# Retention in chunks of 64 tokens on 64x64 quarters of the array, in a kernel that fuses retention with a gated dense layer

## The chip, the cores and the metric

The kernel runs on one core of one Trainium2 chip. The metric is the device time of one execution in microseconds (us); lower is better. "The profiled span" is the length of one execution in the hardware profile; it is about 1 to 2 us shorter than the time of the same run. "The granted clock" is the share of its full clock that TensorE was allowed to use.

## The reference

Eight sequences of 576 tokens, eight heads of 64 dimensions. Each head computes causal attention without softmax, weighted by a decay, and a dense layer of 512 to 2048 to 512 with the gate h·cos(h) follows:

```python
gamma = 1.0 - 2.0 ** (-5.0 - np.arange(H))
rel   = pos[:, None] - pos[None, :]
Dmat  = np.where(rel >= 0, gamma[:, None, None] ** rel[None], 0.0)
x     = ((q @ k.T) / sqrt(64) * Dmat) @ v        # per head; x is (4608, 512)
h     = x @ w_in                                 # 512 -> 2048
out   = (h * np.cos(h)) @ w_out                  # 2048 -> 512
```

The decay factors into a power for the query and one for the key. So a block of tokens needs only its own masked scores, and one 64x64 *state* per head (the sum of k·v over all earlier tokens of the sequence) for everything before it.

## The kernel before

The 4608 tokens are taken in 36 groups of 128. One group's retention consists of *scores* (k·q), a mask on VectorE, the *own* products (v times masked scores), the *carried* products (state times q), and *states* (k·v, for the next group). A sequence has 576 = 4.5 x 128 tokens, so every ninth group holds the end of one sequence and the start of another; it needs a "mixed" mask (`tri_mix`) and a copy of v with half the rows cleared (`v_odd`).

The groups are packed into stages n0 to n9 of 512 (n1, n2: 256) tokens of the dense layer. In n3 to n9 the second dense product is Strassen's: seven products of quarter size, numbered 1 to 7, on sums of gate blocks ("gate sums", mostly on GpSimd) and of weight blocks. The work of two groups is slipped between two of these products, twice per stage. I call such a piece of work a *unit*.

```python
def scores(g, bank, ...):                  # shortened
    for hg in range(HG):
        for he in range(2):                # 64 rows x 128 keys, or 64x64 (parts=2), 128 columns
            nc.tensor.matmul(ps[i0:i1, he, hg, :], lhsT=qkT[d0:d0+D, HG+hg, i0:i1],
                             rhs=qT[d0:d0+D, hg, :], start=True, stop=True)
    mask = tri_mix if g % PER == MIX else tri
    # VectorE: ret = ps * mask

def unit7(g, bank, ...):                   # two groups between two dense products
    copy = states([g + 1, g + 2], bank)()  # 128x64 products, state adds on VectorE
    then()
    attn_out([g, g + 1], "m", nc.scalar.copy)      # own (128x64), then carried (64x64)
    if more: scores2(g + 2, put_off)
    copy(nc.scalar.copy)

# ... start-up, groups 0 to 3, before the first dense product
scores(0, "a", idle=2)
for g in range(4):
    ...
    if g + 1 < 4:
        state(g)
        transposes(g + 1, ...)             # TensorE, copied by ScalarE
        scores(g + 1, "ab"[(g + 1) % 2], idle=3)   # next scores, in another bank ...
        attn_out([g], "m", evac=nc.scalar.copy)    # ... ahead of this group's outputs
```

From group 6 on, q and k are transposed by DMA (`qkT<-qks`).

Of the kernel before, what the change touches and what calls it, by code (L numbers as in the profile page):

```python
# [17 lines left out]
def kernel(  # L18
# [28 lines left out]
    HP = P // 2  # L47
    gammas = [1.0 - 2.0 ** (-5.0 - h) for h in range(H)]
# [8 lines left out]
    S7 = 3  # L57
# [7 lines left out]
    retp = ctx.enter_context(tc.tile_pool(name="retp", bufs=4))  # L65
# [22 lines left out]
    tri = consts.tile([P, P], F32)  # L88
    tri_mix = consts.tile([P, P], F32)
    diag2 = consts.tile([P, P], F32)  # L90
# [5 lines left out]
    v_odd = consts.tile([P, 2, H, D], BF16)  # L96

    blocks4 = [consts.tile([P, HG, D], BF16, tag=f"sb{x}", name=f"sb{x}") for x in range(4)]

    tiles = {}  # L100

    def head(he, hg):
        return he * HG + hg

    def load(g, names="qkv", gate=None):

        t0 = g * P
        if g % PER == MIX:
            parts = [(0, HP, t0), (HP, P, t0 + HP)]
        else:  # L110
            parts = [(0, P, t0)]
        for name in names:
            src = {"q": q, "k": k, "v": v}[name]
            f = ld.tile([P, H, D], F32, tag="f" + name, name=f"f{name}")
            for p0, p1, t in parts:
                b, s0 = divmod(t, S)
                i = nc.sync.dma_start(
                    f[p0:p1], src[b, :, s0 : s0 + p1 - p0, :].rearrange("h s d -> s h d")
                )
                if gate is not None:  # L120
                    tc.add_manual_dep(
                        i.ins, gate.ins.name,
                        mybir.DependencyInfo(
                            mybir.DependencyClass.Sync, mybir.DependencyReason.DATA
                        ),
                        reason="weights first",
                    )
                    gate = None
            tiles["f" + name, g] = f

    def prep(g, early=False, kv_first=False):
# [22 lines left out]
        else:  # L154
            copy_v = nc.scalar.copy if g > starts[S7] // P + 17 else nc.gpsimd.tensor_copy
            copy_v(vb, fv)  # L156
            if c == MIX and g > PER:
                copy_v(v_odd[HP:, g // PER % 2], fv[HP:])
# [28 lines left out]
    def scores(g, bank, idle=0, parts=1, put_off=None):  # L187
        qks, vb, qkT, qT = tiles["a", g]
        ps = psum.tile([P, 2, HG, P], F32, tag=bank, name="sc")
        warm(ps[:, 0].rearrange("p b i -> p (b i)"), idle)  # L190
        for hg in range(HG):
            for i0 in range(0, P, P // parts):
                for he in range(2):
                    d0, i1 = he * D, i0 + P // parts
                    nc.tensor.matmul(  # L195
                        ps[i0:i1, he, hg, :],
                        lhsT=qkT[d0 : d0 + D, HG + hg, i0:i1],
                        rhs=qT[d0 : d0 + D, hg, :],
                        start=True,
                        stop=True,  # L200
                    )
        ret = retp.tile([P, 2, HG, P], BF16, tag="ret", name="ret")
        mask = tri_mix if g % PER == MIX else tri
        tiles["ret", g] = ret

        def masked():
            nc.vector.tensor_tensor(  # L207
                out=ret.rearrange("p a b i -> p (a b) i"),
                in0=ps.rearrange("p a b i -> p (a b) i"),
                in1=mask.unsqueeze(1).to_broadcast([P, H, P]),  # L210
# [3 lines left out]
        if put_off is None:  # L214
            masked()
        else:
            put_off.append(masked)

    def state(g):
        c = g % PER  # L220
        if c == PER - 1:
            return
        qks, vb, qkT, qT = tiles["a", g]
        fresh = c in (0, MIX)
        if fresh:
            tiles["stps"] = psum.tile([P, HG, P], F32, tag="st", name="st")
        ps = tiles["stps"]
        p0 = HP if c == g == MIX else 0
        vs = v_odd[:, g // PER % 2] if c == MIX and g > PER else vb
        for hg in range(HG):  # L230
            nc.tensor.matmul(
                ps[:, hg, :],
                lhsT=qks[p0:, 1, 2 * hg : 2 * hg + 2, :].rearrange("s h d -> s (h d)"),
                rhs=vs[p0:].rearrange("s (a b) d -> s b a d", a=2)[:, hg],
                start=(fresh and hg == 0),
                stop=(c in (MIX - 1, PER - 2) and hg == HG - 1),
                skip_group_check=True,
            )
        sb = stp.tile([P, HG, P], BF16, tag="sb", name="sb")
        nc.vector.tensor_tensor(  # L240
            out=sb,
            in0=ps,
            in1=diag2.unsqueeze(1).to_broadcast([P, HG, P]),
            op=ALU.mult,
        )
        tiles["sb", g + 1] = sb

    def states(gs, bank="st"):



        gs = [g for g in gs if g < NG and g % PER != PER - 1]
        if not gs:
            return lambda: (lambda *_: None)
        apart = bank == "b"
        if apart:
            two = psum.tile([P, 2, 2, HG, D], F32, tag=bank, name="st")
            ps = two[:, :, 0]
        else:
            ps = psum.tile([P, len(gs), HG, D], F32, tag=bank, name="st")  # L260
        for x, g in enumerate(gs):
            qks, vb, qkT, qT = tiles["a", g]
            vs = v_odd[:, g // PER % 2] if g % PER == MIX else vb
            for hg in range(HG):
                for he in range(2):
                    nc.tensor.matmul(
                        ps[he * D : he * D + D, x, hg, :],
                        lhsT=qks[:, 1, 2 * hg + he, :],
                        rhs=vs[:, head(he, hg), :],
                        start=((apart or x == 0) and hg == 0),  # L270
                        stop=((apart or x + 1 == len(gs)) and hg == HG - 1),
                        skip_group_check=True,
                    )

        def copy(run=nc.vector.tensor_copy):
            for g in gs:
                s, sb = tiles.pop(("s32", g)), blocks4[g % 4]
                run(sb, s)
                tiles["sb", g + 1] = sb

        def add():
            for x, g in enumerate(gs):
                s = stp.tile([P, HG, D], F32, tag="s32", name="s32")
                if g % PER in (0, MIX):
                    nc.vector.tensor_copy(s, ps[:, x])
                else:
                    nc.vector.tensor_tensor(out=s, in0=ps[:, x], in1=tiles["s32"], op=ALU.add)
                tiles["s32"] = tiles["s32", g] = s
            return copy

        return add

    def attn_out(gs, bank, evac=nc.vector.tensor_copy):


        two = len(gs) == 2
        ps = psum.tile([P, DG, len(gs), P], F32, tag=bank, name="ov")

        def out_of(h, x, n=P):
            return ps[h % 2 * D : h % 2 * D + D, h // 2, x, :n]  # L300

        def carried():
            for h0 in (0, 2) if two else (0,):
                for x, g in enumerate(gs):
                    c = g % PER
                    if c == 0:
                        continue
                    qT = tiles["a", g][3]
                    sb = tiles["sb", g]
                    n = HP if c == MIX else P  # L310
                    heads = [(he, h0 + j) for j in range(2) for he in range(2)]
                    if not two:
                        heads = [(he, hg) for hg in range(HG) for he in range(2)]
                        heads.sort(key=lambda u: head(*u))
                    for he, hg in heads:
                        h = head(he, hg)
                        r = slice(he * D, he * D + D)
                        k = r if two else slice(0, P)
                        nc.tensor.matmul(  # L319
                            out_of(h, x, n),  # L320
                            lhsT=sb[k, hg, r] if sb.shape[2] == P else sb[k, hg, :],
                            rhs=qT[k, hg, :n],
                            start=(not two and h < 2),
                            stop=(two and h % HG >= 2),
                            skip_group_check=True,
                        )

        def own():
            for x, g in enumerate(gs):
                vb = tiles["a", g][1]  # L330
                ret = tiles.pop(("ret", g))
                for h in range(H):
                    nc.tensor.matmul(  # L333
                        out_of(h, x),
# [547 lines left out]
```

## Time and profile before

| | before |
|---|---|
| time, median of the first 3 runs | 299.27 us (298.97 to 299.58) |
| profiled span | 296.6 us |
| TensorE matmul busy | 285.2 us, 96% |
| VectorE, GpSimd, ScalarE busy | 70%, 67%, 46% |
| granted clock | 1.00 |

Of the waits of TensorE before, two lines (engine and tile waiting, what it waited for, us in total, times, longest):

```profile
PE sc L195 <- DMA qkT<-qks: 1.2, 1, 1.2
PE o L515 <- DVE ot L557: 1.0, 4, 0.4
```

The start-up before, from the timeline of TensorE (start, busy us, line, operation, operands, count, and in brackets the idle time before with what ended it); the lines between are left out. Scores of groups 0 to 3 begin at 9.77, 12.12, 14.52, 16.72, and the first dense product, `h`, at 17.61:

```profile
9.77 0.45 PE L195 MATMUL sc<-qT,qkT 64*128 64x128 bf16 x8 [0.25 <-ACT qkT L177]
12.12 0.40 PE L195 MATMUL sc<-qT,qkT 64*128 64x128 bf16 x8
...
17.61 1.05 PE L365 MATMUL h<-xT,w_in_sb 128*128 128x256 bf16 x8
...
19.49 0.71 PE L365 MATMUL h<-xT,w_in_sb 128*128 128x256 bf16 x5
```

One unit before, in stage n6, from the same view. It runs from 193.79 to 195.28:

```profile
193.79 0.32 PE L266 MATMUL st<-vb,qks 128*64 128x64 bf16 x8
193.94 0.62 PE L333 MATMUL ov<-ret,vb 128*64 128x128 bf16 x16
194.49 0.42 PE L319 MATMUL ov<-qkT,sb 64*64 64x128 bf16 x16
194.73 0.62 PE L195 MATMUL sc<-qkT 64*64 64x128 bf16 x32
195.28 1.92 PE L515 MATMUL o<-w_out_sb,gT 128*128 128x256 bf16 x16
```

The last transposing DMA that n5 needs was issued at 160.91, and the unit whose scores need it began at 163.55. The lead was 2.6 us. The scores of the unit's second group, which need this DMA, began at 164.94, and the DMA had landed at 164.90. The issue and the scores, from the timelines of the DMA queue (SPq) and of TensorE (the second group is the second half of the scores' line):

```profile
160.91 1.29 SPq L167 DMA_TRANSPOSE qkT<-qks  x1
164.62 0.74 PE L195 MATMUL sc<-qkT 64*64 64x128 bf16 x32
```

### The profile page before, as it was taken

Reading aid. Unit: us, or ns where it says so; the run is one execution under the profiler, and the core shown is the slowest. Engines: PE = TensorE matmul, PEld = TensorE weight load, DVE = VectorE, ACT = ScalarE, POOL = GpSimd, SP = SyncE. Lnnn points to the kernel's source line nnn. Section 1 sums busy time; section 2 is a strip of 40 time slices with the busy share of each in tenths; the row PEclk is TensorE's granted clock in tenths of the full one; section 3 lists DMA queues with packets and bytes.
Section 4 is the critical chain, followed back from the end, with each engine's and each line's share of the span. In section 5 each row is a group of like instructions: output and inputs, shape, how many; then the busy total and the mean of one; then the engine's idle time right before and its main releaser. Section 6 shows DMA issues by size and latency. Waiting matters only on the chain. (4 is left out here: it accounts for less than half of the span.)

```text
span 296.6 us, 7311 instructions
## 1 busy us (share of the span) xinstructions
PE 285.2 (96%) x3091; PEld 195.6 (66%) x3113; DVE 208.9 (70%) x245; ACT 135.9 (46%) x167; POOL 199.7 (67%) x163
## 2 busy tenths in 40 slices
PE   7899999999989999999999999999999999999995
PEld 3478646848568887468745784488448844884594
DVE  6677647564669995688758975897589758935873
ACT  3656432605236532663256355636464446425620
POOL 2750056544445789999999998599859935970583
PEclk9999999999999999999999999999999999999999
DMA  8999999999999999999999999997850260021013
GB/s 208 213 210 207 210 197 201 210 210 232 201 160 232 199 243 231 216 283 160 198 217 254 212 213 221 200 223 194 180 140 2 73 144 0 2 81 62 0 38 106
DMA packets 154304, 50.28 MB, mean 170 GB/s; under 512 B 140832, under 2 KB 153248, under 8 KB 154272
## 3 DMA queue, kind: packets, MB, share of 16 engines
q1 hardware_dynamic: 149504, 45.10, 77.9%
q0 software_dynamic: 4224, 4.19, 8.5%
q8 instruction: 24, 0.39, 0.5%
q10 hardware_dynamic: 544, 0.52, 0.5%
q14 instruction: 8, 0.07, 0.1%
HBM read 36.70 MB, written 9.44 MB: 156 GB/s over the span
## 5 line engine op out<-in xcount | busy, mean ns | idle before, releaser
L443 POOL TENSOR_TENSOR gs<-gT 128x1024 bf16<-128x1024 bf16 x51 | 107.1, 2131 | 36.1 <-DVE gs L443 35.5
L365 PE MATMUL h<-xT,w_in_sb 128*128 128x512 bf16 (+2 forms) x820 | 126.8, 313 | 1.3 <-DVE xT L350 0.7
L374 DVE TENSOR_TENSOR gT<-h,cosh 128x1024 bf16<-128x1024 f32 x72 | 87.9, 1223 | 45.5 <-ACT cosh L373 43.0
L373 ACT ACTIVATE cosh<-h,half_pi 128x1024 f32<-128x1024 f32 x72 | 80.2, 1114 | 66.9 <-PE h L365 66.9
L365 PEld LDWEIGHTS <-w_in_sb 128*128 128x128 bf16 x832 | 75.9, 98 | 49.5 <-issue 1.0
L140 POOL TENSOR_TENSOR qks<-fq,gq 128x512 bf16<-128x512 f32 x32 | 34.2, 1068 | 40.0 <-DMA fq<-in_q_dram 33.7
L515 PEld LDWEIGHTS <-gs 128*128 128x128 bf16 x576 | 53.9, 98 | 9.5 <-issue 1.7
L140 POOL TENSOR_TENSOR qks<-fk,gk 128x512 bf16<-128x512 f32 x35 | 37.7, 1076 | 9.4 <-DMA fk<-in_k_dram 8.8
L207 DVE TENSOR_TENSOR ret<-sc,tri 128x1024 bf16<-128x1024 f32 x32 | 38.1, 1215 | 2.7 <-PE sc L195 2.7
L515 PE MATMUL o<-ws,gs 128*128 128x256 bf16 (+1 forms) x352 | 38.8, 268 | 0.1
L382 PE MATMUL o<-w_out_sb,gT 128*128 128x512 bf16 x120 | 28.9, 380 | 0.5 <-issue 0.2
L515 PE MATMUL o<-w_out_sb,gs 128*128 128x256 bf16 x224 | 26.3, 272 | 1.0 <-DVE ot L557 1.0
L515 PE MATMUL o<-w_out_sb,gT 128*128 128x256 bf16 x224 | 26.3, 273 | 0.0
L535 DVE TENSOR_TENSOR ot<-o,ot 128x512 f32<-128x512 f32 (+2 forms) x25 | 14.9, 603 | 13.9 <-PE o L515 13.8
L515 PEld LDWEIGHTS <-gT 128*128 128x128 bf16 x224 | 21.5, 98 | 4.2
L350 ACT CAST xT<-ov 128x1024 bf16<-128x1024 f32 (+1 forms) x18 | 16.5, 917 | 16.0 <-PE ov L319 13.9
L443 DVE TENSOR_TENSOR gs<-gT 128x1024 bf16<-128x1024 bf16 (+1 forms) x18 | 21.1, 1187 | 0.3
L382 PEld LDWEIGHTS <-gT 128*128 128x128 bf16 x128 | 11.8, 98 | 12.5
L156 POOL CAST vb<-fv 128x512 bf16<-128x512 f32 x22 | 13.8, 628 | 5.1 <-DMA fv<-in_v_dram 3.3
L562 ACT COPY ot<-o 128x512 f32<-128x512 f32 x7 | 4.1, 586 | 20.2 <-PE o L515 20.2
L392 ACT COPY ot<-o 128x512 f32<-128x512 f32 x8 | 4.7, 588 | 18.5 <-PE o L382 18.4
L195 PEld LDWEIGHTS <-qkT 64*64 64x64 bf16 (+1 forms) x512 | 9.0, 105 | 6.1 <-ACT qkT L177 2.3
(70 smaller groups left out, 176.1 us busy)
## 6 DMA issues: line engine op xcount, KB each, us to landing
out_dram<-ot SPq DMA_DIRECT2D x35, 256.0 KB, 4.0
fk<-in_k_dram SPq DMA_DIRECT2D x32, 256.0 KB, 5.1
fv<-in_v_dram SPq DMA_DIRECT2D x32, 256.0 KB, 5.1
fq<-in_q_dram SPq DMA_DIRECT2D x30, 256.0 KB, 4.5
w_in_sb<-in_moe_w_in_dram POOLq DMA_DIRECT2D x4, 512.0 KB, 8.9
w_out_sb<-in_moe_w_out_dram POOLq DMA_DIRECT2D x4, 512.0 KB, 16.3
fq<-in_q_dram SPq DMA_DIRECT2D x8, 128.0 KB, 4.0
fk<-in_k_dram SPq DMA_DIRECT2D x8, 128.0 KB, 4.1
```

The lines of the kernel that those rows point to most:

```text
L140: eng.tensor_tensor(out=qks[:, m].rearrange("p (b a) d -> p a b d", a=2), in0=f.rearrange("p (a b) d -> p a b d", a=2), in1=by[:, c, :].re ...
L156: copy_v(vb, fv)
L195: nc.tensor.matmul(ps[i0:i1, he, hg, :], lhsT=qkT[d0 : d0 + D, HG + hg, i0:i1], rhs=qT[d0 : d0 + D, hg, :], start=True, stop=True,)
L207: nc.vector.tensor_tensor(out=ret.rearrange("p a b i -> p (a b) i"), in0=ps.rearrange("p a b i -> p (a b) i"), in1=mask.unsqueeze(1).to_br ...
L350: evac(tiles["x", n][:, :, t0 : t0 + len(gs) * P], ps.rearrange("p c x i -> p c (x i)"))
L365: nc.tensor.matmul(ps[:, j, :], lhsT=w_in_sb[:, dg, (et + j) * P : (et + j + 1) * P], rhs=xT[:, dg, c0 : c0 + w], start=(dg == 0), stop=(d ...
L373: nc.scalar.activation(cosh, ps, ACTF.Sin, bias=half_pi, scale=1.0)
L374: nc.vector.tensor_mul(gT[:, et : et + m, c0 : c0 + w], ps, cosh)
L382: nc.tensor.matmul(ps, lhsT=gT[:, et, tsi * P : (tsi + 1) * P], rhs=w_out_sb[:, et, :], start=(et == 0), stop=(et == ET - 1),)
L443: i = (nc.vector if on_dve else nc.gpsimd).tensor_tensor(out=tiles["gs", n, x][:, e0:e1], in0=i0, in1=i1, op=op_)
L515: nc.tensor.matmul(dst[i], lhsT=lhs[:, e, j * P : (j + 1) * P], rhs=rhs[:, e, c0:c1], start=(x in (3, 4, 1, 7) and e == 0 and (i == 0 or l ...
L535: pend.append(lambda: nc.vector.tensor_tensor(out=out_, in0=in0, in1=in1, op=op_))
```

## The change

Intent: 576 is nine times 64. In chunks of 64 tokens no chunk straddles two sequences, so the mixed masks go. A mask covers 64 by 64, so VectorE masks half as many elements. And every product is 64x64 with 64 columns: four of them run in the four quarters of the array, and the tile shape no longer changes within a unit. Between products that use different rows for the same output an order must be kept; this is done with an empty instruction (nop) on ScalarE. The diff, cut to its core:

```diff
-    def scores(g, bank, idle=0, parts=1, put_off=None):
+    def scores(gs, bank="a", idle=0):
+        for y, g in enumerate(gs):
+            for hg in range(HG):
+                for x in range(2):
+                    for he in range(2):
+                        nc.tensor.matmul(ps[half(x), he, y, hg, :],
+                            lhsT=qkT[half(he), HG + hg, half(x)],
+                            rhs=qT[half(he), hg, half(x)], start=True, stop=True)
...
+    def retention(gs, bank="m", evac=nc.scalar.copy, between=lambda: None):
...  (cut: the products are sorted into three parts: carried, own, carried of the other row half)
+        for p, part in enumerate(parts):
+            for h, x, y, lhsT, rhs in part:
+                i = nc.tensor.matmul(ps[half(h % 2), x, y, h // 2, :], lhsT=lhsT, rhs=rhs, ...)
+                if turn is not None:
+                    fence(i, turn, "other rows")
+                    turn = None
+            if p == 0:
+                if i is not None:
+                    turn = nc.scalar.nop()
+                    fence(turn, i, "other rows")
+                between()                  # scores and states of the next pair
...
     # start-up
-    scores(0, "a", idle=2)
     for g in range(G4):
+        masked = scores([g], idle=2)
...
+        add, copy = states([2 * g, 2 * g + 1])
+        add(0, 1)
+        copy(0, 1, nc.vector.tensor_copy)
+        masked()
+        add(1)
+        copy(1)                            # ScalarE
         if g + 1 < G4:
-            state(g)
-            transposes(g + 1, "nn", only=(1,))
-            scores(g + 1, "ab"[(g + 1) % 2], idle=3)
-            attn_out([g], "m", evac=nc.scalar.copy)
+            transposes(g + 1, (("n", "st")[g % 2],) * 2, only=(1,))
+            retention([g])
...
+    def unit(g, bank="m", more=True, then=lambda: None, finish=at_once):
+        found = []
+        more = more and g + 2 < NG
+        retention([g, g + 1], bank,
+            between=lambda: found.extend(ready([g + 2, g + 3])) if more else None)
+        then()
+        if more:
+            finish(*found)
```

So a steady unit's order changes from states, own, carried, scores to carried, scores, states, own, carried. One gate sum of the stages n5 to n8 also moves from GpSimd to VectorE.

## The prediction

> **What bounds the kernel.** The busy table gives TensorE matmul 285.2 of 296.6 us (96%); VectorE 70%, GpSimd 67%, ScalarE 46%. The waits of TensorE add up to about 6 us; the granted clock is 1.00. So after the prelude (17.6 us, latency bound) TensorE time is kernel time. The dense products (110 ns per 256 columns) are not touched.
>
> **What retention costs now.** In the timeline the work of one steady pair of 128-token groups stands at 193.79 to 195.28: states 0.15 to 0.27, own 0.55, carried 0.25, scores 0.55. It delays TensorE by about 1.58 us between the products around it; 18 pairs, some 27 us. Starts in the trace: four 64x64 matmuls of 128 columns every 56 ns; four of 64 columns (mixed groups, one sample) 28 ns; their weight loads also 28 to 31 ns. Each change of tile shape shows about 0.1 us extra, three to four per pair. The Trainium skill, "TensorEngine Tiling (Array Packing)", Key Properties, says that a mode change drains TensorE; the gaps agree.
>
> **What the change does to TensorE.** Per pair 32 scores, 32 states, 32 own, 32 carried, all 64x64 with 64 columns: 4 x 8 quads x 31 ns = 1.0 us, plus two mode changes: estimate 1.25 us against 1.58, so 0.33 saved per pair where nothing waits; at best 6 us.
>
> **What takes it back.**
> - The fence through a ScalarE nop should pass once earlier ScalarE work is dispatched (Trainium skill, "PSUM — Partial Sum Buffer", Engine vs sequencer instructions). With scores and states between (0.5 us) it is free; without, I estimate 0.33 us of stall (groups 3, 4, 5, some pairs).
> - States now take bank b directly after product 3 of a stage: they must wait for VectorE's last gate product (193.30 to 194.52). Estimate 0.3 us in each of the last four stages with retention, which eats that unit's gain.
> - In the prelude retention(g) precedes scores(g+1): 0.3 us later.
> - Pair 10/11 waits for its transposing DMA (1.16 us now); more work follows that wait: 0.25 us lost.
>
> **What else is gained.** Product 2's wait for VectorE's "ot" (0.16 to 0.38 us per stage, 1.0 in all) goes, since one mask (1.21 us) per pair leaves VectorE, against two more state adds (0.42) and a gate sum from GpSimd (2.13 there). The waits of scores for "s" (0.45) and states for "ot" (0.28) go. VectorE falls by about 10 us, GpSimd by 6 to 10; neither is critical.
>
> **Sum.** Last four stages with retention 1.7, 117 to 148 us 1.0, 85 to 117 us 1.2, before that 0, prelude -0.3: 3.5 us saved. Predicted 295.8 us (-1.2%), 8 in 10 within 293.0 to 298.4. Faster by over 2%: 0.12; within 2%: 0.85; slower by over 2%: 0.03.
>
> **What would show it.** Scores, states, own, carried: mean start pitch 7 to 8 ns per matmul, no 128x64 forms left. TensorE busy down by 4 to 6 us. Waits list: states waiting for the gate product (L374), 0.3 us each; own products waiting for ScalarE only where nothing lies between; product 2's wait for "ot" gone. First h matmul at about 18 us.
>
> **What would make it wrong.** Quads of 64 columns held by weight loads (over 40 ns a quad takes all the gain); the nop queuing behind running ScalarE work (Sin 1.11 us), up to 1 us per unit and then slower; or bank b free early, 1.2 us more gain.

## More of the kernel before

A function `feed`, called after each output store, issues on the queue of SyncE the loads of q, k, v some groups ahead, and the transposing DMAs, one behind the other. GpSimd scales q and k and casts v before that.

From the page of the kernel before: the busy table, TensorE's clock and the DMA's busy share in 40 slices of the span, and the queue that carries instructions.

```profile
span 296.6 us, 7311 instructions
PE 285.2 (96%) x3091; PEld 195.6 (66%) x3113; DVE 208.9 (70%) x245; ACT 135.9 (46%) x167; POOL 199.7 (67%) x163
PEclk9999999999999999999999999999999999999999
DMA  8999999999999999999999999997850260021013
q8 instruction: 24, 0.39, 0.5%
```

TensorE is busy nearly always, so it bounds the kernel. But look at the DMA row too: it stands at 90% or more in 26 of the first 27 slices.

The busy times by stretch, of n4 and n5 before (length, then busy us and count of TensorE, weight loads, VectorE, ScalarE, GpSimd; clock; DMA busy share; GB/s).

```profile
116.87:147.85 30.98, 30.36 (x352) 19.97 (x353) 23.39 (x25) 13.61 (x16) 30.07 (x24) 1.00 1.10 215
147.85:178.09 30.24, 29.75 (x336) 19.94 (x337) 23.16 (x24) 15.92 (x21) 28.84 (x24) 1.00 1.12 225
```

GpSimd, 67% busy over the span, is busy 30.07 of 30.98 us in n4.

## The result, and the profile after

| | before | after |
|---|---|---|
| time, median (range) of 4 runs each | 299.42 us (298.97 to 301.03) | 310.01 us (309.73 to 310.21) |
| ratio of the fast runs | | 1.0343, 95% interval 1.0303 to 1.0383 |
| profiled span | 296.6 us | 308.1 us |
| TensorE matmul busy | 285.2 us | 284.3 us |
| granted clock, mean | 1.00 | 0.971 |

All runs of this table gave correct results. Ratios here and below are the mean time of one kernel's fast runs over that of the other's in the same rounds, so they are not quite the ratio of the medians quoted. The change is 3.4% slower; 310 lies far outside the range predicted.

The same lines of the page, after (the DMA row, again full, is left out):

```profile
span 308.1 us, 9160 instructions
PE 284.3 (92%) x3982; PEld 194.6 (63%) x4006; DVE 197.2 (64%) x259; ACT 147.0 (48%) x184; POOL 190.3 (62%) x158
PEclk9857999999999999999999979999999999999999
q8 instruction: 31, 0.51, 0.8%
```

TensorE's busy time did not rise; its idle time did, by 12.4 us (23.8 against 11.4). VectorE and GpSimd have less to do, as intended. The clock row has two dips that were not there. And the instruction queue moved 31 packets instead of 24. Of the waits of TensorE after, those that bear on what follows:

```profile
PE sc L190 <- DMA qkT<-qks: 5.7, 2, 3.7
PE ov L300 <- ACTq L314: 2.4, 4, 0.8
PE o L492 <- POOL gs L422: 2.3, 4, 1.0
PE h L344 <- DVE ret L202: 1.6, 1, 1.6
PE st L234 <- DVE gT L353: 0.6, 3, 0.2
```

To place the loss I took from both traces the start of each stage, that is of its first weight load for a dense product (to within 0.1 us). "Full h" is the point from which the dense products of n0 run without a break (19.49 before). All in us of the profiled runs:

| | start to full h | n0 | n1 | n2 | n3 | n4 | n5 | n6 | n7 | n8 |
|---|---|---|---|---|---|---|---|---|---|---|
| before | 19.49 | 29.32 | 17.47 | 18.62 | 31.97 | 30.98 | 30.24 | 29.69 | 29.75 | 29.10 |
| after | 26.85 | 29.42 | 17.34 | 18.38 | 32.60 | 32.42 | 34.14 | 29.03 | 29.03 | 28.78 |
| difference | +7.36 | +0.10 | -0.13 | -0.24 | +0.63 | +1.44 | +3.90 | -0.66 | -0.72 | -0.32 |

So there are three parts: a gain of 1.70 in n6 to n8, a loss of 7.36 in the start-up, and a loss of 5.97 in n3 to n5. (n9 holds no unit and hardly moved; the columns sum to +11.4 of the 11.5 us between the spans.)

**The gain.** One unit after, n6, the counterpart of the unit shown above:

```profile
206.91 0.32 PE L300 MATMUL ov<-qkT,sb 64*64 64x64 bf16 x16
207.05 0.43 PE L190 MATMUL sc<-qkT 64*64 64x64 bf16 x32
207.69 0.37 PE L234 MATMUL st<-vb,qks 64*64 64x64 bf16 x20 [0.21 <-DVE gT L353]
...
207.95 0.43 PE L300 MATMUL ov<-ret,vb 64*64 64x64 bf16 x28
208.20 0.33 PE L300 MATMUL ov<-qkT,sb 64*64 64x64 bf16 x16
208.46 1.92 PE L492 MATMUL o<-w_out_sb,gT 128*128 128x256 bf16 x16
```

The states wait 0.21 us for the last gate product, and this unit takes 208.46 - 206.91 = 1.55 us, about what it took before. The other unit of the stage waits for nothing and takes 1.23 us, from its first product to the next dense one, where one before took some 1.5:

```profile
213.80 0.28 PE L300 MATMUL ov<-qkT,sb 64*64 64x64 bf16 x10
215.03 1.70 PE L492 MATMUL o<-ws,gs 128*128 128x256 bf16 x14
```

Product 2 no longer waits for "ot". This part works as predicted.

**The start-up.** From the same timeline, lines between left out:

```profile
10.04 0.50 PE L190 MATMUL sc<-qT,qkT 64*64 64x64 bf16 x16 [0.24 <-ACT qkT L172]
12.72 0.32 PE L300 MATMUL ov<-ret,vb 64*64 64x64 bf16 x16 [0.74 <-ACTq L314]
13.59 0.35 PE L190 MATMUL sc<-qT,qkT 64*64 64x64 bf16 x16 [0.16 <-ACT qkT L172]
16.37 0.43 PE L300 MATMUL ov<-ret,vb 64*64 64x64 bf16 x16 [0.67 <-ACTq L314]
...
21.89 0.43 PE L190 MATMUL sc<-qT,qkT 64*64 64x64 bf16 x16 [0.36 <-ACT xT L328]
24.14 1.86 PE L344 MATMUL h<-xT,w_in_sb 128*128 128x256 bf16 x8 [1.61 <-DVE ret L202]
```

Of the rounds left out, the scores begin at 17.80 and the own products at 20.45. One round from scores to scores took 2.2 to 2.4 us before; now it takes 3.6, 4.2 and 4.1. Own products wait each time for the nop ("ACTq" is ScalarE's queue). The first group of eight dense products takes 1.86 us instead of 1.05: the clock is halved. In the record of the clock it stands at 0.5 from 13.7 to 27.4 us. (The expectations of e1 and e7 below put this stretch at 6.8 to 20.5 us; that was misread.)

ScalarE at the first of these nops:

```profile
12.65 0.41 ACT L258 CAST sb<-s 128x256 bf16<-128x256 f32 x1 [2.14 <-DVE s L252]
```

The nop stands behind the cast of the second state. The cast begins at 12.65, and the own products at 12.72, while the cast still runs until 13.06. At the other two nops it is the same: the trace has the nops at 12.66, 16.31 and 20.39, and the casts' starts at 12.65, 16.30 and 20.34. So the nop passes as soon as the cast has been *dispatched*. This agrees with the Trainium skill, "PSUM — Partial Sum Buffer", Engine vs sequencer instructions, which says that the sequencer waits only for earlier instructions to be dispatched. The prediction cited that sentence and drew the wrong conclusion from it: the cast could not be dispatched before VectorE's fourth operation of the round (the add of the second state, 12.20 to 12.61) was done. A nop behind an instruction that waits for another engine waited for that engine too.

One more link stands in the last line of TensorE's timeline above. The first dense product waits 1.61 us for VectorE's mask of group 3. The code says why: all scores of the new start-up use bank "a", which the first dense product takes too; before, they alternated between "a" and "b", and no such wait is in that trace.

**The transposing DMA in n5.** TensorE after, around the longest wait (before, the scores of the counterpart began at 164.62 without a wait):

```profile
172.73 0.32 PE L300 MATMUL ov<-qkT,sb 64*64 64x64 bf16 x16
172.87 0.30 PE L190 MATMUL sc<-qkT 64*64 64x64 bf16 x16
176.91 0.32 PE L190 MATMUL sc<-qkT 64*64 64x64 bf16 x16 [3.74 <-DMA qkT<-qks]
...
178.01 3.36 PE L492 MATMUL o<-w_out_sb,gT 128*128 128x256 bf16 x16
```

The DMA that the second half of these scores needs was issued at 172.80 after (160.91 before), as the timeline of the DMA queue says:

```profile
172.80 1.38 SPq L162 DMA_TRANSPOSE qkT<-qks  x1
```

The unit began at 172.73. The lead of 2.6 us had become -0.1. The wait costs more than itself: after 3.7 us of idling the clock halves again, and the next product takes 3.36 us instead of 1.91. That queue hardly stands still: from the first transposing DMA to this one no gap is longer than 1.3 us in either kernel. The first one was issued 5.4 us later than before (55.58 against 50.17), and the stretch from there to this one was 6.5 us longer (117.2 against 110.7), as much as its loads of q, k and v held the queue longer (65.8 against 59.3 us). So the issue was late in part because the start was, in part because the loads were slower.

And the new units need the DMA sooner. In the old order the second group's scores began 1.39 us after the unit (164.94 against 163.55). In the new order they would have begun after 0.44 us (176.91 less the wait of 3.74 is 173.17, against 172.73). So of the wait of 3.74 us, 0.95 comes from the new order within the unit and 2.7 from the lost lead.

**Gate sums.** The same stretches as shown before, after (n4 and n5):

```profile
124.59:157.01 32.42, 30.04 (x481) 19.71 (x481) 24.64 (x30) 15.53 (x18) 29.72 (x24) 1.00 1.09 200
157.01:191.15 34.14, 30.30 (x417) 20.29 (x417) 20.80 (x26) 16.66 (x21) 31.84 (x27) 0.95 1.16 216
```

GpSimd works 29.7 us in n4, as before, but with its inputs later: in this stretch it waits 2.0 us for loads of q and v (0.3 us before). A GpSimd without slack then hands its gate sums over late, and the last products of n3 and n4 wait 0.2 to 1.0 us each, four times, 2.3 in all.

### The profile page after: what moved, and what is told of

It is laid out like the page before. It is cut to its first block, busy times and chain, and to the rows that moved or that the text cites. A ratio compares the mean times of both kernels' runs of the same rounds, so it can differ in the third digit from the quotient of the medians.

```text
span 308.1 us, 9160 instructions
## 1 busy us (share of the span) xinstructions
PE 284.3 (92%) x3982; PEld 194.6 (63%) x4006; DVE 197.2 (64%) x259; ACT 147.0 (48%) x184; POOL 190.3 (62%) x158
## 4 chain that ended last, share of the span: by engine, by line
PE 66%; POOL 9%; DMA 8%; DVE 5%; issue 4%; ACT 4%; SPq 2%; DVEq 0%; ACTq 0%; POOLq 0%
PE h L344 34%; PE o L492 18%; PE o L361 7%; POOL gs L422 7%; DMA fq<-in_q_dram 5%; DMA qkT<-qks 3%; PE ov L300 3%; ACT cosh L352 2%; PE idle L180 2%; POOL qks L137 2%; DVE gT L353 2%; PE st L234 1%; SPq L120 1%; PE sc L190 1%; DVE s L252 1%
## 5 line engine op out<-in xcount | busy, mean ns | idle before, releaser
L422 POOL TENSOR_TENSOR gs<-gT 128x1024 bf16<-128x1024 bf16 x47 | 98.6, 2128 | 48.5 <-DVE gs L422 48.5
L258 ACT CAST sb<-s 128x1024 bf16<-128x1024 f32 (+3 forms) x20 | 16.6, 832 | 39.3 <-DVE s L252 34.3
L252 DVE TENSOR_TENSOR s<-st,s 128x256 f32<-128x256 f32 x56 | 23.6, 422 | 14.6 <-PE st L234 13.5
L512 DVE TENSOR_TENSOR ot<-o,ot 128x512 f32<-128x512 f32 (+2 forms) x32 | 19.7, 622 | 18.8 <-PE o L492 15.4
L492 PE MATMUL o<-w_out_sb,gT 128*128 128x256 bf16 x224 | 28.1, 282 | 0.7 <-DVE gT L353 0.7
L331 ACT CAST xT<-ov 128x512 bf16<-128x512 f32 x30 | 16.1, 589 | 21.4 <-PE ov L300 21.0
L202 DVE TENSOR_TENSOR ret<-sc,tri 128x1024 bf16<-128x1024 f32 (+1 forms) x21 | 22.3, 1064 | 5.1 <-PE sc L190 5.1
L422 DVE TENSOR_TENSOR gs<-gT 128x1024 bf16<-128x1024 bf16 (+1 forms) x22 | 18.8, 879 | 0.4
L512 DVE TENSOR_TENSOR ot<-ot,o 128x512 f32<-128x512 f32 x14 | 9.6, 687 | 7.4 <-ACT ot L542 4.5
```

The source lines that it names most:

```text
L202: nc.vector.tensor_tensor(out=ret[:, :, : len(gs)].rearrange("p a g b i -> p a (g b) i"), in0=ps[:, :, : len(gs)].rearrange("p a g b i -> ...
L252: nc.vector.tensor_tensor(out=s32[:, y], in0=kv[c], in1=tiles["s32"], op=ALU.add)
L258: run(sb[:, y0:y1], s32[:, y0:y1])
L331: evac(xT[:, x], ps[:, x])
L422: i = (nc.vector if on_dve else nc.gpsimd).tensor_tensor(out=tiles["gs", n, x][:, e0:e1], in0=i0, in1=i1, op=op_)
L492: nc.tensor.matmul(dst[i], lhsT=lhs[:, e, j * P : (j + 1) * P], rhs=rhs[:, e, c0:c1], start=(x in (3, 4, 1, 7) and e == 0 and (i == 0 or l ...
```

## The experiments

Theory 1: the start-up's loss is a serial chain, TensorE states, VectorE add, ScalarE cast, nop, own products, and the next scores behind all that. Rival 1: the halved clock makes it long. Theory 2: the losses in n3 to n5 (n2 to n5 where the start-up is the old one) come from the loads. The change has about 1800 more TensorE instructions, these are fetched by DMA in packets, and the packets hold up a load stream that has no slack. Rival 2: these losses come from the late start alone, or from the new units themselves (their order, as just seen, does take a part).

All twelve kernels gave correct results. The kernel before, run beside them, had medians of 299.25 to 299.61 us (one of its runs, beside e4, e7 and e12, was slow and is left out of the ratios).

### e1: the second cast on VectorE; e2: scores ahead; e3: both

e1 takes the cast away from ScalarE, e2 puts the scores of the next group ahead of the retention of this one as the kernel before had it (with it the scores alternate between two banks again, behind three idle products instead of two), e3 does both.

```diff
 e1, e3:
-        copy(1)
+        copy(1, run=nc.vector.tensor_copy)
 e2, e3:
+    nxt = scores([0], idle=2)
     for g in range(G4):
-        masked = scores([g], idle=2)
+        masked = nxt
...
-        add, copy = states([2 * g, 2 * g + 1])
+        add, copy = states([2 * g, 2 * g + 1], ("n", "st"))
...
-            transposes(g + 1, (("n", "st")[g % 2],) * 2, only=(1,))
+            to = "ba"[g % 2]
+            transposes(g + 1, to + to, only=(1,))
+            warm(psum.tile([P, 512], F32, tag="m", name="idle"), 3)
+            nxt = scores([g + 1], to)
             retention([g])
```

> The changed kernel with one line altered: in the prelude the bf16 cast of the second state runs on VectorE instead of ScalarE. Theory A (the nop and the next qkT copy queue on ScalarE behind that cast, which waits for the fourth VectorE op): the wait of own products for the nop falls from 0.7 us per group to under 0.2, scores(3) start at about 19.5 instead of 21.9 us, first full h at about 24.3 instead of 26.85, total 307.0 to 307.8 (changed: 310.0). Rival B (it is the order, retention(g) ahead of scores(g+1)): under 0.7 us gained, 309.4 or more. Rival C (the halved clock from 6.8 to 20.5 us is the cause): unchanged, 310.

> The changed kernel with the kernel before's order in the prelude: transposes and scores of the next group ahead of retention of this one; the ScalarE cast stays. Theory A: the next qkT copy still queues behind the cast on ScalarE, so scores(g+1) gain little by the order: 1 to 2 us gained, 308 to 309. Rival B (order alone): most of the 7.4 us of the prelude comes back, 302.5 to 304.

> Both edits. Both theories: the prelude is as short as before's within 1.5 us, full h stream from 20 to 21 us instead of 26.85. If the later losses (stages at 92 to 191 us: +0.6, +1.4, +3.9 us) are only a result of lateness of the prelude, they go too and the total is 293 to 297, faster than before (299.4). If they come from the changed steady part itself, the total is 302 to 304.

| | time, us | ratio to before | full h at | end of n0 at |
|---|---|---|---|---|
| after | 310.01 | 1.0343 (1.0303 to 1.0383) | 26.85 | 56.27 |
| e1 | 309.75 | 1.0357 (1.0300 to 1.0414) | 25.58 | 56.32 |
| e2 | 309.43 | 1.0346 (1.0303 to 1.0389) | 25.56 | 55.89 |
| e3 | 307.35 | 1.0278 (1.0246 to 1.0310) | 22.52 | 52.58 |

The expectations missed in size. Full h was to come at 24.3 us in e1 and at 20 to 21 in e3. No total lies in a range given for theory A (theory 1 here), e3's lies outside both of its ranges, and e1's, taken alone, would fit rival B. (e1 and e2 have two runs each.) So the chain is read from the traces, not from the totals. Each edit alone moves full h by 1.3 us, and in the total neither shows. Together they move it by 4.3 us. That is what two links of one serial chain do: take one away and the other stands in its place. In e1 the own products wait for VectorE's mask instead (0.9 us, three times), in e2 the scores wait for ScalarE's copy of the keys (3.1 us, four times). The first dense product's wait for the mask is still there in e1 (1.6 us) and gone in e2 and e3, which alternate the banks. e1's own gain is then lost in n0 (30.74 us against 29.42): the half-clock stretch lasted 17.1 us there and reached into the dense products. e3's profile (of the fastest of its six runs, 304.36 us) has nearly the same losses in n3 to n5, 5.1 us, with 4.2 us of waits for transposing DMAs and 2.2 us for gate sums, though full h comes 4.3 us earlier. So most of them do not come from the start-up's length; e6 tests this better.

### e4: the nop on VectorE

```diff
-            retention([g])
+            retention([g], by=nc.vector)      # turn = by.nop() in place of nc.scalar.nop()
```

> The kernel after, with one difference: in the start-up alone, the empty instruction that separates the carried products from the own products stands on VectorE instead of ScalarE. Theory (the empty instruction waits its turn behind ScalarE's cast of the second state, 0.74, 0.67 and 0.77 us of TensorE wait): those three waits fall to 0.1 to 0.4 us, but the copy of the next transposed keys on ScalarE still stands behind the same cast, so the first full dense product moves only 0.5 to 1.3 us earlier than 26.85. Rival (the fence itself, wherever it stands, drains TensorE): waits and start-up unchanged. In either case the time stays above 308.

308.13 us, 1.0285 (1.0249 to 1.0321). The three waits fell to 0.35, 0.27 and 0.28 us and are now put down to VectorE's mask. So the nop's place cost the wait, not the fence as such. But full h came at 26.53, only 0.3 us earlier, less than the theory's 0.5 to 1.3: the time went into the next link. I expected the direction and over-estimated the size.

### e7: idle products against the halved clock

```diff
-            retention([g])
+            retention([g], between=lambda: warm(
+                psum.tile([P, 512], F32, tag=("st", "n")[g % 2], name="idle"), 4))
```

> The kernel after, with four idle 128x512 products put into the gap between carried and own products of each of the three start-up retentions (0.86 us of TensorE work at full clock). It asks what the granted clock of 0.5 between 6.8 and 20.5 us costs. If the clock is what makes the start-up long, the half-clock period vanishes or shrinks and the first full dense product comes 1.5 us or more earlier than 26.85. If the chain through ScalarE and VectorE is what makes it long, the clock rises but the start-up stays within 0.7 us of 26.85, or gets longer by what the idle products overshoot the gap.

The clock stays at 1.0 through the whole start-up; the page's clock row, which can be held against that of the kernel after:

```profile
PEclk9997999999999999999999779999999999999999
```

The first dense product comes at 23.71 instead of 24.14, 0.4 us earlier, and full h 1.3 us earlier, because those eight products now take 1.03 us. This fits neither of my bounds. But at the end of n0 only 0.3 us is left of it (56.00 against 56.27): a half-clock stretch of 3.4 us came all the same, now in the first dense products, where 12 ran at 0.21 us apiece instead of 0.11. So rival 1 falls as the main cause. The clock costs something, but with a full clock the start-up is still over 6 us longer than before.

The kernel as a whole was 305.11 us, 1.0200 (1.0160 to 1.0240), nearly 5 us faster than the change, though the start-up cannot account for that. (The profiled run is the slowest of the four, 306.94 us.) I come back to that below.

### e6: the old start-up with the new rest

The start-up of before, up to group 3, with its own scores, states and outputs; everything after it as in the kernel after (some 80 lines of the old kernel put back, with its 128x128 mask and `diag2`).

> The changed kernel with the first four groups done as in the kernel before (128-token chunks, masks and state bank as there), all later groups in 64-token chunks. Full h stream at 19.4 to 19.8 us as before. Theory L (the later losses are only lateness of the prelude): stages at or below before's, total 293 to 296. Theory I (TensorE's 1500 extra instructions are fetched by DMA in 16 KB packets, 30 instead of 24, and each stalls the saturated load stream by 1.3 us): the stage after the fifth (30.24 us in before, 34.1 in changed) still loses 2 to 4 us on the transposing DMA, total 297 to 300.

Two of the four runs were slow (307.68 and 305.99); the fast ones are 303.71 and 301.41, ratio 1.0114 (1.0046 to 1.0183). Both are slower than the 297 to 300 that I expected with theory I (theory 2 here), and the four runs lie far apart. Full h came at 19.44, as before. So the whole 7.4 us belong to the new start-up. The later losses stay, and the waits of its TensorE show them undiluted:

```profile
PE sc L192 <- DMA qkT<-qks: 7.9, 3, 4.0
PE o L560 <- POOL gs L490: 3.0, 4, 1.0
```

The two long waits for transposing DMAs stand in n2 (3.96 us) and n5 (3.47 us). Against before, n2, n4 and n5 lose 3.2, 1.4 and 2.9 us. Stages n6 to n8 are as in the kernel after (29.03, 29.03, 28.78). So the middle stages lose with the old start-up too.

### e5: the old kernel, started late

The first half of rival 2. The kernel before, with 30 idle products (6.45 us) before the dense part:

```diff
+    warm(psum.tile([P, 512], F32, tag="n", name="idle"), 30)
     for g in (4, 5):
         prep(g)
```

> The kernel before with 30 idle matmuls of 512 columns (6.5 us) put ahead of its first h matmul, nothing else. If lateness by itself upsets the later stages (loads held back, then late), the total rises by clearly more than 6.5 us: 308 to 311, and the trace shows new waits for transposing DMAs or gate sums between 90 and 190 us. If lateness alone is harmless, 305.5 to 306.3 and the later stages keep their lengths (31.9, 31.0, 30.2 us).

306.85 us, 1.0260 (1.0209 to 1.0311), between my two ranges. The profiled span grew by 7.7 us, of which 6.45 is the delay. Beyond it, n3 and n4 took 2.8 us more (33.57 and 32.17 us against 31.97 and 30.98, with 2.3 us of waits for VectorE's gate product), and n2 took 1.35 us less, as its wait for a DMA vanished. But n5 took 30.08 us, and no wait for a late transposing DMA appeared there: the unit began 7.9 us later than before (171.44), the DMA was issued 4.8 us later (165.75), so the lead grew. A late start alone does not make n5's wait.

### e8: the old kernel with more TensorE instructions

The test of theory 2 itself: the kernel before, its dense products of 256 and 512 columns cut into two halves. The same arithmetic, the same loads, the same retention.

```diff
+            k = 2 if w > P else 1
             for dg in range(DG):
-                nc.tensor.matmul(ps[:, j, :], lhsT=..., rhs=xT[:, dg, c0 : c0 + w], ...)
+                for z in range(k):
+                    nc.tensor.matmul(ps[:, j, z * w // k : (z + 1) * w // k], lhsT=..., 
+                        rhs=xT[:, dg, c0 + z * w // k : c0 + (z + 1) * w // k], ...)
...                                            # and likewise in mm2
```

> The kernel before with most dense products cut into two half-width matmuls: 1664 more TensorE instructions, the same arithmetic, no other change. By the pitches in the trace (216, 109, 56 ns for 512, 256, 128 columns) this costs TensorE 2.3 us. Theory I: 30 or 31 instruction packets instead of 24, load issues take 4 to 6 us longer between the first and the 18th transposing DMA, and a new wait for that DMA shows near 165 us: total 303 to 306. Rival (instruction count is harmless): total 301 to 302.3, no such wait.

304.08 us, 1.0167 (1.0126 to 1.0208), profiled span 303.1. From its page and its waits:

```profile
PE 291.4 (96%) x3945; PEld 251.4 (83%) x3945; DVE 211.4 (70%) x245; ACT 136.0 (45%) x167; POOL 199.0 (66%) x163
q8 instruction: 30, 0.49, 0.7%
...
PE sc L195 <- DMA qkT<-qks: 2.4, 2, 1.7
PE o L520 <- POOL gs L448: 1.0, 2, 0.7
```

The old kernel, without any change of its retention, gets the symptoms of the new one: 30 packets, a wait of 1.71 us for a transposing DMA in n5 (33.17 us long instead of 30.24), gate sums that come late in n4. The cut products cost something on TensorE too: in the stages without such waits (n0, n1, n6 to n8) the kernel lost 0.9 us in all. In n2 to n5 it lost 5.5 us (18.39, 33.00, 32.78, 33.17). There TensorE's idle time rose by some 2.2 us and its busy time by 3.4, of which about 1.7 can be the clock, which stands at 0.5 for 3.4 us from 171.0 us on, just behind the wait in n5. So I estimate that about 3.9 of the 5.5 us are waiting and what it brings, and 1.6 the cut products' own cost. The profiled run is the slowest of four; two others had a granted clock of 0.999 and 1.000 and still took 303.74 and 303.32 us, so the slowdown of 4 us does not hang on the halved clock.

What the packets do can be counted in the traces. Between the first and the 18th transposing DMA of a kernel stand the loads of q, k and v that decide when those DMAs are issued. I took how long the queue was held by each load (half of them between 0.6 and 1.1 us), how many packets of instructions started in between, and how long the stretch lasted:

| | matmuls and weight loads, page | packets in all | packets in the stretch | loads held over 1.9 us | all loads, us | stretch, us |
|---|---|---|---|---|---|---|
| before | 6204 | 24 | 10 | 2 | 59.3 | 110.7 |
| e5 | - | 24 | 10 | 3 | 60.8 | 113.5 |
| after | 7988 | 31 | 14 | 7 | 65.8 | 117.2 |
| e6 | - | 30 | 13 | 5 | 63.6 | 116.7 |
| e8 | 7890 | 30 | 14 | 5 | 63.2 | 116.7 |
| e7 | - | 31 | 14 | 2 | 62.6 | 115.3 |

A packet is 16 KB (0.39 MB / 24). The Trainium skill, "Runtime: NRT & Kernel Launch", Instruction fetch mechanics, says that instructions are refilled in blocks of 16 KiB, 256 instructions each, through DMA. The traces agree: 6204 / 256 = 24.2 and 7988 / 256 = 31.2, against 24 and 31 packets. The same section calls the cost of a block mostly hidden. For the loads that share the DMA engines it is not: over all fourteen kernels, of 245 loads with a packet started between 1.0 us before and 1.5 us after their own start, 59 were held over 1.9 us. Of 655 without one, 1 was. With the packets' times shifted by 3 us either way, the same count gives 4 of 290 and 2 of 292. The mean load took 1.26 us near a packet and 0.84 elsewhere. I estimate from each kernel's own means that the loads near packets held the queue for 9.8 us more than they would have elsewhere in the kernel after, for 4.8 before, but for only 6.8 in e8. Over all kernels that is 0.4 to 0.8 us a packet, not the 1.3 that I expected in e6. So packets can explain most of the longer stretch of the kernel after (6.5 us) and about half of what e8's loads took longer (3.9 us).

e7 shows how much hangs on where the packets fall. It has as many of them as the change, but a few dozen more instructions in its start-up (9208 in all against 9160) shift all later packets against the stream. One load in the queue of the kernel after, and the same one in e7 (another, at 48.90 after, went from 2.30 to 0.85 us):

```profile
58.98 2.67 SPq L120 DMA_DIRECT2D fv<-in_v_dram  x1
```

```profile
57.07 0.92 SPq L120 DMA_DIRECT2D fv<-in_v_dram  x1
```

Its wait in n2 is gone (16.27 us against 18.38), that in n5 is 2.8 us. That these hits were missed *because* the packets shifted is the reading that I find likely. No run moves the packets and nothing else, so this much is argued, not shown. And it does not reach n5: with two loads held instead of seven, n5 still took 34.28 us, no less than the 34.14 of the kernel after, as a half-clock stretch of 6.8 us came with the wait. So held loads alone do not make n5's loss.

### e9 to e12: can the saturated stream be relieved?

If transposing DMAs stand behind loads that are not needed yet, those loads can be issued later. e9 is e6 with loads kept three groups ahead instead of five at four places:

```diff
+            if (n, r) in ((0, 3), (1, 0), (1, 1), (1, 2)):
+                ahead = prepared + 3
             while loaded < min(NG, prepared + LD, ahead):
```

> As e6_old_prelude, and around the fourth and fifth stage the loads are issued three groups ahead instead of five, so that the two transposing DMAs that the fifth stage waits for stand earlier in their queue. If theory I and the queue order hold, the wait of 3 to 4 us is gone and the total is 2 to 4 us below e6_old_prelude, 293 to 296, faster than before; if the wait has another cause, it is within 1 us of e6_old_prelude.

300.69 us, 1.0028 (0.9968 to 1.0089): the best version of the new retention, and level with before; the 293 to 296 that I expected were missed. n5 fell from 33.17 to 29.08 us; its wait is gone, with the number of instructions unchanged. Its DMA was issued at 159.62, 8.7 us before the unit began. This shows that with an early issue n5 loses nothing; it is 1.2 us shorter than before. But n6 rose by 1.6 us (three short waits) and n4 to 33.25, where the products wait 3.0 us for gate sums.

e10 adds two more reliefs to e9: the preparation of pair 10/11 at the end of n2, where its DMA has landed, and one gate sum of n4 on VectorE. It holds loads back at three places only.

```diff
-            if (n, r) in ((0, 3), (1, 0), (1, 1), (1, 2)):
+            if (n, r) in ((0, 3), (1, 0), (1, 1)):
...
-            (S7, 1, 4), (last, 1, 0), (last, 2, 4)
+            (S7, 1, 4), (S7 + 1, 2, 4), (last, 1, 0), (last, 2, 4)
...
-            todo = [..., (25, lambda: unit(8))]
+            todo = [..., (25, lambda: unit(8, more=False)), (31, lambda: first(*ready([10, 11])))]
```

> e9_old_prelude_loads_later with three reliefs: loads held back only up to the fifth transposing DMA of that stretch; scores and states of groups 10 and 11 issued at the end of the third stage instead of inside the unit of groups 8 and 9 (their transposing DMA was waited for 3.6 us there); one gate sum of the fifth stage on VectorE instead of GpSimd (GpSimd sums were waited for 3.0 us there). If those three waits are the rest of the loss and the 64-token units keep their gain: 294.5 to 297, faster than before by 0.8 to 1.6%. If the saturated DMA stream only moves the waits elsewhere: 298.5 to 301.

A miss: 302.79 us, 1.0119 (1.0088 to 1.0149). n2's wait fell (3.6 to 1.4 us) and n4 came down to 30.71. But VectorE got the mask and four state adds just before the first gate products of n3, and n3 rose to 35.14. The traces show the chain of the start-up again: VectorE was done with the adds at 87.26, ScalarE's cast of the states waited for them until 87.29, the cosine of n3's first products stood behind the cast (88.72), the gate product behind the cosine (89.87), and the dense products of 91.15 waited 1.74 us for the gate product, and a half-clock stretch of 3.4 us came with it.

And with the fourth place not held back, n5's wait returned (2.7 us in two waits, n5 33.47).

e11 is the control: the kernel before with the same three places held back.

> The kernel before with only the later loads of e10. It waits for no transposing DMA of that stretch, so the relief alone should buy nothing: within 1 us of before (299.3). If it is faster by 1.5 us or more, part of e10's gain is not the chunks' doing.

299.39 us, 1.0001 (0.9976 to 1.0026). Later loads alone buy nothing where nothing is late.

e12 is e9 with the one gate sum of n4 on VectorE.

> The kernel e9 (start-up of before, rest of after, four load batches later) with one GpSimd gate sum of stage n4 (product 2, second half) put on VectorE, which in e10 took n4 from 33.25 to 30.71. Prediction: n4 30.5 to 31.5, the other stages as in e9 (n5 29.1, n2 21.4); in all 297.5 to 299.5, that is 0.0 to 0.6 per cent below before. If saturated engines only pass the wait on, n4 gains and n5 or n6 lose as much, and the time stays at 300 to 301.

A miss again: 300.71 us, 1.0048 (1.0012 to 1.0084). n4 came to 31.87, n5 stayed at 29.18, and n6 stood at 30.94. No version of the new retention that I tried beats the kernel before.

## Why the prediction was wrong, point by point

- *"After the prelude TensorE time is kernel time"* failed, and it is the step on which the rest stood. TensorE's busy time was to fall by 4 to 6 us. It fell by 0.9, because it rose by 2.7 in the start-up, much of which ran at half clock, and the kernel became 10.6 us slower. There was a second limit just below the first: a load stream almost without gaps from 50 to 170 us, whose lead of 2.6 us in n5 was all used, and GpSimd at 97% in n4 (30.07 of 30.98 us). I read the shares over the whole span (GpSimd 67%) and wrote "neither is critical". Stage by stage it is.
- *The term "prelude -0.3"*, a loss of 0.3 us, measured 7.4. The term counted one reordering. It left out that own products, the next keys' copy and the next scores all came to stand behind the second cast, and that this cast waits for VectorE. e6 gives the 7.4 back as a whole; e1, e2 and e3 show the chain (1.3, 1.3, together 4.3); e4 and e7 show that neither the fence's engine nor the clock is the main part. The chain was shown link by link only as far as e3; what makes up the remaining 3.0 us between e3 and the old start-up I have not taken apart.
- *"117 to 148 us 1.0, 85 to 117 us 1.2"*, gains of 2.2 us in n4 and n3, became losses of 1.4 and 0.6 us. The new waits of n4 are for gate sums of GpSimd (2.1 us), which had its inputs later; those of n3 are mostly for VectorE's gate product (0.7 us) and of a kind that the trace does not explain (0.5 us).
- *"Pair 10/11 ... 0.25 us lost"* was right in kind: that wait grew from 1.16 to 1.96 us. But the same kind of wait, 3.7 us, appeared in n5, where I looked for a gain. I looked only at waits that were already there, and not at a lead that was used up to 0.04 us, nor at the new order, which puts the scores 0.95 us nearer to the unit's start.
- *Additional instructions.* The prediction costed 64x64 products by TensorE time alone. It did not cost the 1784 more instructions as 7 more packets on the DMA engines. e8 puts nearly as many into the old kernel and gets the late DMA and the late gate sums. How much of the 6.0 us in n3 to n5 is due to packets, and how much to the later start and the new order, stays open: e5 shows that a late start alone costs 1.3 us beyond itself, without n5's wait, and e7 that n5 loses as much with few loads held.
- *"Last four stages with retention 1.7"*: three of them, n6 to n8, gave 1.70 us; the fourth, n5, lost 3.90. The mechanism is right. The 64x64 products of 64 columns start every 9 ns (28 own products from 207.95 to 208.20), there is no form change left within a unit, and the states wait 0.2 us for the gate product (predicted 0.3) three times. The Trainium skill, "TensorEngine Tiling (Array Packing)", Key Properties, says that a change of tiling mode drains TensorE; the unit's fall from about 1.5 to 1.23 us, with the arithmetic spread over 120 products instead of 72, agrees with it, but no run here isolates the drain.
- *"First h matmul at about 18 us"* was given as a check. It came at 24.14 and would have shown the error at once.
- *"The nop queuing behind running ScalarE work"* was named as a risk, for the steady units. There it cost nearly nothing; it came in the start-up, and not behind running work but behind work that waited.

## What to carry to other kernels

Before you call an engine or the DMA uncritical, read its busy share stage by stage and the lead with which its results arrive, and when you reorder work, what the new order asks for sooner; an engine at 67% overall can have no slack in the one stage that matters. Cost a change that multiplies small instructions twice, once on the engine that runs them and once on the DMA engines that fetch them, if loads already fill those engines (how much of this loss the second item made is not settled here). And in a latency-bound start-up write down the chain of engines for one round: an instruction that only orders two others can inherit the waits of the queue that it stands in, as the nop did here.

## What the Trainium skill lacked or had wrong

- "Runtime: NRT & Kernel Launch", Instruction fetch mechanics, calls the cost of a 16 KiB block mostly hidden. It lacks that the block takes room from a saturated load stream: 59 of 245 loads close to a packet held the queue for over 1.9 us, against 1 of 655 others; half of all loads take 0.6 to 1.1 us.
- "PSUM — Partial Sum Buffer", Engine vs sequencer instructions, is right that a nop waits only for dispatch (own products at 12.72 us, 0.07 us after the cast before the nop began and 0.34 us before it ended). The section lacks that the nop also waits with an earlier instruction that itself waits for another engine (0.67 to 0.77 us of TensorE's time here).
- "TensorE: Matmul & The Clock Gate", What's actually happening, says that the clock halves after an idle window of about 3.4 us. The traces agree only in part. A wait of 3.74 us halved the clock in the kernel after, but so did waits of 1.71 us in e8 (n5) and 1.74 us in e10 (n3), and a wait of 3.47 us in e6 (n5) did not. The page says that the clock follows how busy TensorE was, but not how much is enough: from 17.5 to 24.1 us TensorE was busy for 3.2 of 6.6 us in the start-up after, and the clock stayed at 0.5; with the idle products of e7, busy for 3.3 of 4.0 us from 16 to 20 us, it stayed at 1.0, and after 1.8 of 4.0 us from 20 to 24 it halved at 24.8.
- "TensorE: Matmul & The Clock Gate", Wait — 56ns, not 53.3ns?, says that start-to-start never drops below about 25 ns, however few the columns. It does not say there that products in different parts of the array are excepted (the same page, Why this matters for your kernels, has products in distinct row groups start 4 ns apart or less). Here 28 products in quarters of the array, 64x64 with 64 columns, start within 0.25 us, 9 ns apart; a set of four takes 36 ns.
